# A linear-attention and gated-MLP stack on one core: another opening for the first layer, a later denominator sum, and weight-product rows inside the last q unit

## The chip, the cores and the metric

The kernel runs on one core of one Trainium2 chip. The metric is the device time of one execution in microseconds (us), as a median over runs; the kernel before takes 1659.09 us (three runs, 1657.82 to 1659.62). The profiled execution's span, from its first to its last instruction, is some 2 us shorter than the time of the same run, because the time also covers start and end; spans are compared with spans and times with times. A ratio printed with a result is the mean time of one kernel's runs over the mean of the other's of the same rounds, so it is not quite the ratio of the medians that stand beside it.

Engine names: PE is TensorE (matmuls), PEld its weight load, DVE is VectorE, ACT is ScalarE, POOL is GpSimd, SP issues DMAs. PSUM is the memory that matmuls write to; the kernel cuts it into three "mm" buffers and one "kv" buffer. A "bank" in this text is one of these buffers.

## The reference, cut to what matters

Two kinds of layer alternate, A B A B, on 2048 rows of 1024 bf16 values, with the same weights in both rounds.

```python
x = x + A(layernorm(x), wqkv, wo)      # layer 1, and again layer 3
x = x + B(layernorm(x), w_gate, w_up, w_down)   # layer 2, and again layer 4

# A: linear attention, 32 heads of 32
q, k, v = split(x @ wqkv)
phi = lambda t: where(t > 0, t + 1, exp(t)) + 1e-6
kv = einsum("bhsd,bhse->bhde", phi(k), v);  z = sum_s phi(k)
o  = (phi(q) @ kv) / (phi(q) . z + 1e-6);   return o @ wo

# B:  ((x @ w_gate) * (x @ w_up)) @ w_down        (1024 -> 3584 -> 1024)
```

## The kernel before

The kernel never forms v. It computes G = xᵀ·phi(k) (the "Gram units" g, 32 matmuls each), then kv = wvᵀ·G (the "kv units"), masks kv to the heads' diagonal blocks (KVb), and multiplies it by wo to get one 1024×1024 weight M (eight "rows"). An output unit is then one product of the divided phi(q) with M. The sum z over all rows is gathered by DVE in f32 (`z_unit`), split into two bf16 halves (`z_split`) and summed over the partitions by four matmuls with ones (`z_sum`); ACT copies the result to `zacc`, which every division on DVE reads.

In these traces each engine takes its instructions in program order (the run with the old loads, below, shows DVE idle for 2.48 us in front of a copy that could have run). The order in which these units are called is therefore the schedule:

```python
def phi(ps, dst, scale):                       # after every k and q unit
    nc.scalar.activation(out=e, in_=ps, func=Exp)        # ACT
    nc.scalar.activation(out=dst, in_=ps, func=Relu)     # ACT, then PSUM is free
    nc.vector.tensor_scalar(out=e, in0=e, 1.0, EPS, min, add)   # DVE
    nc.vector.tensor_tensor(out=dst, in0=dst, in1=e, op=add)    # DVE

def m_unit(c):                                  # one row of M
    ps = mm_tile(); both(ps, KVb[:, c, :], wo[c], True, True)   # 2 matmuls
    # copy to M: DVE for odd c, ACT for even c

# opening of layer 1 (turn_pe: transpose by PE, ACT copies one half, turn_rest: DVE the other)
idle(9); ln_stats(0); centre(0); turn_pe(0); idle(2)
ln_stats(1, split=lambda: turn_rest(0)); centre(1)
k_part(0, 0, 4); turn_pe(1); turn_rest(1); k_part(0, 4, 6); k_part(1, 0, 6)
ln_stats(2); centre(2); k_part(0, 6, 8); turn_pe(2); turn_rest(2); k_part(1, 6, 8)
ln_stats(3); centre(3); k_part(2, 0, 4); turn_pe(3); turn_rest(3)
k_part(2, 4, 8); k_part(3, 0, 8)
# ... q and k units with norms between them, z_split last ...

# middle of layers 1 and 3; d(t) is a division, 5 DVE instructions
do([g[0], z_sum, g[1], kv[0]] + d(0) + [g[2], kv[1]] + d(1, 2) + [q[0], g[3], kv[2]] + d(3, 4))
do([q[1], g[4], kv[3]] + d(5, 6) + [q[2], g[5], kv[4]] + d(7))
do(d(8) + [q[3], g[6], kv[5]] + d(9, 10) + [q[4], kv[6], q[5]] + d(11) + [g[7]] + d(12))
do([q[6], kv[7], q[7]])
do([m_unit(c) for c in range(KD)])
do([out_unit(0)] + d(13) + [out_unit(1)] + d(14) + [out_unit(2)] + d(15) + [out_unit(3)])
# ... the other output units, woven with the norms of layer B ...
```

(Arguments shortened; `k_part(t, a, b)` multiplies rows a to b of the key weights into tile t.)

Of the kernel before, what the change touches and what calls it, by code (L numbers as in the profile page):

```python
# [8 lines left out]
ACT = mybir.ActivationFunctionType  # L9
ALU = mybir.AluOpType  # L10
AX = mybir.AxisListType
BF16 = mybir.dt.bfloat16
F32 = mybir.dt.float32
# [13 lines left out]
def kernel(  # L27
# [11 lines left out]
    nc = tc.nc  # L39
# [69 lines left out]
    def load_x(t):  # L109
        load(X[:, t, :], x_view[:, t, :])  # L110

    def load_k(a, b):
        load(wkv[:, a:b, :], wqkv_v[:, a:b, D:2 * D])
# [20 lines left out]
    for c in range(2):  # L134
        load(X[:, 0, c * NB:(c + 1) * NB], x_view[:, 0, c * NB:(c + 1) * NB])
    load_x(1)
    for k in range(4):
        load_k(k, k + 1)
    load_x(2)
    for k in range(4, 8):  # L140
        load_k(k, k + 1)
    load_x(3)
    load_q()
    for t in range(4, NT):
        load_x(t)
# [16 lines left out]
    def mm_tile():  # L162
        return psum.tile([P, 2, NB], F32, tag="mm", bufs=3, name="ps")

    def flat(ps):
        return ps[:].rearrange("p a b -> p (a b)")
# [4 lines left out]
    def idle(n):  # L171
        for _ in range(n):
            nc.tensor.matmul(out=zps[:, 0, :], lhsT=xT[3][:, 0, 0:P], rhs=xT[3][:, 0, :], start=True, stop=True)
# [2 lines left out]

    stat = {}

    def ln_stats(t, split=None):
        st = small.tile([P, 2, 6], F32, tag="st", name="st")  # L180
        for c in range(2):
            nc.vector.bn_stats(out=st[:, c, :], in_=X[:, t, c * NB:(c + 1) * NB])  # L182
            if split and c == 0:
                split()
        mv = small.tile([P, 2], F32, tag="mv", bufs=NT, name="mv")
        nc.vector.bn_aggr(out=mv[:], in_=st[:])  # L186
        ve = small.tile([P, 1], F32, tag="ve", name="ve")
        nc.gpsimd.tensor_scalar(out=ve[:], in0=mv[:, 1:2], scalar1=1e-5, scalar2=None, op0=ALU.add)  # L188
        rstd = small.tile([P, 1], F32, tag="rstd", bufs=NT, name="rstd")
        nc.gpsimd.tensor_tensor(out=rstd[:], in0=ve[:], in1=mhalf[:], op=ALU.pow)  # L190
        stat[t] = (mv, rstd)
# [11 lines left out]
    def both(ps, lhsT, rhs, start, stop):  # L203
        for n in range(2):
            nc.tensor.matmul(out=ps[:, n, :], lhsT=lhsT, rhs=rhs[:, n * NB:(n + 1) * NB], start=start, stop=stop)  # L205

    def phi(ps, dst, scale):
        e = small.tile([P, D], BF16, tag="eb", bufs=3, name="e")
        sc = {} if scale is None else {"scale": scale}
        nc.scalar.activation(out=e[:], in_=flat(ps), func=ACT.Exp, **sc)  # L210
        nc.scalar.activation(out=dst, in_=flat(ps), func=ACT.Relu, **sc)
        nc.vector.tensor_scalar(out=e[:], in0=e[:], scalar1=1.0, scalar2=EPS, op0=ALU.min, op1=ALU.add)  # L212
        nc.vector.tensor_tensor(out=dst, in0=dst, in1=e[:], op=ALU.add)  # L213

    def layer_A(li):
        first = li == 0
# [2 lines left out]
        def scale_of(t):  # L219
            return stat[t][1][:] if first and t < TPG else None  # L220
# [3 lines left out]
        def k_part(t, a, b):  # L224
            if a == 0:
                open_ps[t] = mm_tile()
            ps = open_ps[t]
            tl = t % TPG
            for k in range(a, b):
                both(ps, xT[t // TPG][:, k, tl * P:(tl + 1) * P], wkv[:, k, :], k == 0, k == KD - 1)  # L230
            if b == KD:
                phi(ps, PK[:, t, :], scale_of(t))
# [4 lines left out]
        def q_slot(t):  # L237
            return pq[t if t < 8 else t % 4]

        def q_unit(t):  # L240
            def run():
                ps = mm_tile()
                tl = t % TPG
                for k in range(KD):
                    both(ps, xT[t // TPG][:, k, tl * P:(tl + 1) * P], wq[:, k, :], k == 0, k == KD - 1)
                phi(ps, q_slot(t), scale_of(t))
            return run

        def z_unit(t):
# [51 lines left out]
                                                in1=mask[:].unsqueeze(1).to_broadcast([P, 4, P]), op=ALU.mult)  # L301
            return run

        def m_unit(c):
            def run():
                ps = mm_tile()
                both(ps, KVb[:, c, :], wo[c], True, True)
                if c % 2:
                    nc.vector.tensor_copy(out=M[:, c, :], in_=flat(ps))
                else:  # L310
                    nc.scalar.copy(out=M[:, c, :], in_=flat(ps))
            return run

        def out_unit(t):
            def run():
                ps = mm_tile()
                tl = t % TPG
                for c in range(KD):
                    both(ps, xT[t // TPG][:, c, tl * P:(tl + 1) * P], M[:, c, :], c == 0, c == KD - 1)
                nc.vector.tensor_tensor(out=X[:, t, :], in0=X[:, t, :], in1=flat(ps), op=ALU.add)  # L320
            return run
# [10 lines left out]
            return lambda: [z_unit(t)() for t in ts]  # L332

        if first:
            def centre(t):
                nc.vector.tensor_scalar(out=XN[:, t, :], in0=X[:, t, :], scalar1=stat[t][0][:, 0:1], scalar2=None,
                                        op0=ALU.subtract)

            pts = {}

            def turn_pe(t):
                pt = psum.tile([P, KD, P], BF16, tag="mm", bufs=3, name="pt")
                for k in range(KD):
                    nc.tensor.transpose(out=pt[:, k, :], in_=XN[:, t, k * P:(k + 1) * P], identity=ident[:])
                nc.scalar.copy(out=xT[0][:, 0:4, t * P:(t + 1) * P], in_=pt[:, 0:4, :])  # L345
                pts[t] = pt

            def turn_rest(t):
                nc.vector.tensor_copy(out=xT[0][:, 4:8, t * P:(t + 1) * P], in_=pts[t][:, 4:8, :])

            idle(9)
            ln_stats(0)
            centre(0)
            turn_pe(0)
            idle(2)
            ln_stats(1, split=lambda: turn_rest(0))
            centre(1)
            k_part(0, 0, 4)
            turn_pe(1)
            turn_rest(1)  # L360
            k_part(0, 4, 6)
            k_part(1, 0, 6)
            ln_stats(2)
            centre(2)
            k_part(0, 6, 8)
            turn_pe(2)
            turn_rest(2)
            k_part(1, 6, 8)
            ln_stats(3)
            centre(3)  # L370
            k_part(2, 0, 4)
            turn_pe(3)
            turn_rest(3)
            k_part(2, 4, 8)
            k_part(3, 0, 8)
            for t in range(TPG):
                ln_apply(t, XN[:, t, :])
            main = [q_unit(t) for t in range(4)] + [k_unit(t) for t in range(4, 8)] + [q_unit(t) for t in range(4, 8)]
            main += [k_unit(t) for t in range(8, 16)]
            fill = [norm(t) for t in range(4, 16)]  # L380
            fill += [zs(1, 2), zs(3, 4), zs(5, 6), zs(7), zs(8), zs(9), zs(10, 11), zs(12)]
            do(weave(main, fill))
            do([zs(13, 14, 15), z_split])
        else:
            main = [k_unit(t) for t in range(4)] + [q_unit(t) for t in range(4)]
            main += [k_unit(t) for t in range(4, 8)] + [q_unit(t) for t in range(4, 8)]
            main += [k_unit(t) for t in range(8, 16)]
            fill = [norm(t, False) for t in range(12, 16)]
            fill += [zs(1), zs(2), zs(3)] + [lambda: None] * 2
            fill += [zs(4), zs(5), zs(6), zs(7)] + [lambda: None] * 3 + [zs(8), zs(9), zs(10), zs(11)]  # L390
            do(weave(main, fill))
            do([zs(12, 13, 14, 15), z_split])
        load_v()

        def d(*ts):
            return [div_unit(t) for t in ts]

        g, kv, q = ([f(i) for i in range(KD)] for f in (g_unit, kv_unit, lambda i: q_unit(8 + i)))
        do([g[0], z_sum, g[1], kv[0]] + d(0) + [g[2], kv[1]] + d(1, 2) + [q[0], g[3], kv[2]] + d(3, 4))
        do([q[1], g[4], kv[3]] + d(5, 6) + [q[2], g[5], kv[4]] + d(7))  # L400
        load_o(0)
        load_o(1)
        do(d(8) + [q[3], g[6], kv[5]] + d(9, 10) + [q[4], kv[6], q[5]] + d(11) + [g[7]] + d(12))
        do([q[6], kv[7], q[7]])
        do([m_unit(c) for c in range(KD)])
        load_gu(0)
        load_gu(1)
        load_gu(2)
        for j in DN_ORDER[:2]:
            load_dn(j)  # L410
        do([out_unit(0)] + d(13) + [out_unit(1)] + d(14) + [out_unit(2)] + d(15) + [out_unit(3)])
        for j in DN_ORDER[2:6]:
            load_dn(j)
        fill = [lambda t=t: ln_stats(t) for t in range(4)] + [b_norm(t) for t in range(4)]
        do(weave([out_unit(t) for t in range(4, NT)], fill))
        load_dn(DN_ORDER[6])


# [50 lines left out]
    def do(units):  # L469
        for u in units:  # L470
            u()
# [80 lines left out]
```

## Time and profile before

| | before |
|---|---|
| time, median of 3 | 1659.09 us |
| span of the profiled run | 1657.2 us |
| PE busy | 98% of the span |
| PE waits for the first half of the split of z | 6.7 us, 5.1 of them in layer 1 |
| PE waits for centring, transposed tiles and weight rows in the opening | 5.4 us |
| PE waits in the M product, both layers | 3.5 us |

From the page of the kernel before: the busy time of an engine with its share of the span and its instructions, and the chain of work that ended last.

```profile
PE 1627.2 (98%) x7512; PEld 744.8 (45%) x7663; DVE 607.9 (37%) x889; ACT 286.3 (17%) x384; POOL 54.0 (3%) x141
...
PE 90%; DVE 7%; issue 1%; DMA 1%; POOL 1%; ACT 0%; SPq 0%; DVEq 0%; ACTq 0%
```

PE is the bottleneck and is nearly always busy, so only its holes can be won. The share 98% hides them: the chain of work that ended last is on PE for 90% only, and on DVE for 7%. The holes are in the waits view of the kernel before, PE only; its columns are who waited for whom, us in total, how often, and the longest.

```profile
PE ps L205 <- DVE W L256: 6.7, 2, 5.1
PE pt L344 <- DVE R L336: 3.1, 2, 2.8
PE ps L205 <- ACT PQ L211: 2.3, 2, 1.2
PE ps L205 <- ACT xT L345: 1.7, 2, 1.4
...
PE ps L205 <- DVE W L257: 0.7, 2, 0.6
PE ps L205 <- DVE R L309: 0.6, 2, 0.3
PE ps L205 <- ACT R L311: 0.6, 2, 0.3
```

W L256 and L257 are the two halves of the split of z; R L336 is the centring of a tile in the opening and xT L345 ACT's half of a transposed tile; PQ L211 is the Relu of the last phi(q) before the M rows, R L309 and L311 the copies of M's rows. Where these waits lie is in the timeline of PE in the kernel before (start, duration, line, operands, count, and in brackets the idle time before it and what ended it):

```profile
17.23 1.90 PE L205 MATMUL ps<-W,xT 128*128 128x512 bf16 x8 [1.45 <-ACT xT L345]
21.95 1.03 PE L344 MATMUL pt<-ident,R 128*128 128x128 bf16 x8 [2.81 <-DVE R L336]
...
99.12 7.32 PE L205 MATMUL ps<-R,R 128*128 128x512 bf16 x31
111.58 1.01 PE L205 MATMUL ps<-W,ones 128*128 128x512 bf16 x2 [5.14 <-DVE W L256]
112.74 1.01 PE L205 MATMUL ps<-W,ones 128*128 128x512 bf16 x2 [0.15 <-DVE W L257]
...
122.19 0.61 PE L295 MATMUL kv<-GL,W 128*128 128x128 bf16 x8
...
190.94 0.61 PE L295 MATMUL kv<-GL,W 128*128 128x128 bf16 x8
...
197.02 0.59 PE L205 MATMUL ps<-W,KVb 128*128 128x512 bf16 x2 [1.16 <-ACT PQ L211]
...
257.86 27.79 PE L437 MATMUL ps<-xT,R 128*128 128x512 bf16 x125
```

The first Gram unit starts at 99.12; a kv unit follows at 122.19, 23.1 us later. The first Gram unit's own matmuls take 6.9 us of this. The other 36 matmuls of 512 columns take 0.2157 us each when nothing waits, 7.8 us, but 16.2 us pass. From the last kv unit (190.94) to the first matmul of layer B (257.86) 66.9 us pass for 62.6 us of work.

A hole is followed by a second loss. The windows view of the kernel before, cut where the granted clock changes in the trace: the stretch, its length, busy time of PE and the other engines (instruction counts in brackets), the granted TensorE clock, DMA share and GB/s. The pairs are a stretch of 3.41 us and the one after it.

```profile
18.07:21.48 3.41, 1.06 (x5) 0.29 (x3) 2.60 (x6) 1.13 (x2) 0.03 (x1) 1.00 1.06 387
21.49:24.90 3.41, 2.96 (x13) 1.59 (x14) 0.82 (x2) 0.59 (x1) 1.04 (x2) 0.50 1.03 378
...
110.24:117.06 6.82, 5.33 (x13) 1.85 (x14) 4.57 (x5) 1.01 (x1) 0.00 (x0) 0.50 0.01 4
195.57:198.98 3.41, 1.61 (x7) 0.49 (x6) 2.40 (x4) 3.23 (x4) 0.00 (x0) 1.00 1.07 364
198.99:202.39 3.40, 3.40 (x9) 1.22 (x8) 2.23 (x3) 1.90 (x2) 0.00 (x0) 0.50 1.10 350
```

After a stretch in which PE stood still for half of the time or more, the clock is 0.50 for the next 3.41 us (6.8 us after the long hole at the z sum).

### The profile page before, as it was taken

How to read it: one execution, taken by the hardware profiler on the slowest of the kernel's cores; microseconds unless marked ns; L12 is line 12 of the kernel's file. 1: busy time of each engine (PE TensorE's matmuls, PEld its weight loads, DVE VectorE, ACT ScalarE, POOL GpSimd, SP SyncE). 2: the span in 40 equal slices, each digit the busy share in tenths (PEclk: the TensorE clock that was granted, in tenths of full speed). 3: DMA queues.
4: the chain of work that ended last, by engine and by line, in shares of the span. 5: the costliest groups of instructions: out<-in, count | busy, mean ns of one | idle time of the engine just before them, and what ended most of it. 6: DMA issues, size and time to landing. Idle time of an engine off the chain costs nothing.

```text
span 1657.2 us, 17618 instructions
## 1 busy us (share of the span) xinstructions
PE 1627.2 (98%) x7512; PEld 744.8 (45%) x7663; DVE 607.9 (37%) x889; ACT 286.3 (17%) x384; POOL 54.0 (3%) x141
## 2 busy tenths in 40 slices
PE   8989999999999999999999999999999999999999
PEld 3434444444444444444444444444444444444444
DVE  5797782311321231143345687532113113211111
ACT  4532301100110110011035322011001101100110
POOL 1100000000000000010000000000000000000000
PEclk9999999999999999999999999999999999999999
DMA  6322683630551363043420247555215504521400
GB/s 209 64 64 47 183 247 115 177 115 1 171 159 51 90 175 118 0 153 102 77 76 1 70 96 225 158 156 165 84 64 151 179 26 143 167 84 64 153 0 26
DMA packets 234686, 182.56 MB, mean 110 GB/s; under 512 B 100080, under 2 KB 215408, under 8 KB 234608
## 3 DMA queue, kind: packets, MB, share of 16 engines
q1 hardware_dynamic: 234608, 181.43, 37.5%
q8 instruction: 60, 0.98, 0.2%
q14 instruction: 18, 0.15, 0.0%
HBM read 153.09 MB, written 4.19 MB: 95 GB/s over the span
## 4 chain that ended last, share of the span: by engine, by line
PE 90%; DVE 7%; issue 1%; DMA 1%; POOL 1%; ACT 0%; SPq 0%; DVEq 0%; ACTq 0%
PE ps L437 46%; PE ps L205 42%; DVE GL L252 1%; DVE st L182 1%; PE ps L464 1%; DVE R L213 1%; DVE X L320 0%; DVE den L272 0%; DVE PQ L276 0%; PE kv L295 0%; POOL rstd L190 0%; DVE PQ L213 0%; DVE tmp L270 0%; DVE e L212 0%; DVE R L195 0%
## 5 line engine op out<-in xcount | busy, mean ns | idle before, releaser
L437 PE MATMUL ps<-xT,R 128*128 128x512 bf16 x2380 | 525.8, 379 | 2.8
L437 PEld LDWEIGHTS <-R 128*128 128x128 bf16 x2432 | 238.0, 98 | 287.0
L441 DVE TENSOR_TENSOR R<-gs,ps 128x512 bf16<-128x512 f32 x224 | 153.8, 687 | 533.6 <-ACT gs L440 533.6
L205 PEld LDWEIGHTS <-R 128*128 128x128 bf16 x2248 | 220.4, 98 | 266.6 <-issue 3.1
L440 ACT COPY gs<-ps 128x512 f32<-128x512 f32 x224 | 131.3, 586 | 1044.5 <-PE ps L437 1021.6
L437 PE MATMUL ps<-xT,W 128*128 128x512 bf16 x1133 | 250.6, 379 | 1.0
L205 PEld LDWEIGHTS <-xT 128*128 128x128 bf16 x1536 | 149.8, 98 | 184.2 <-issue 5.3
L205 PE MATMUL ps<-W,xT 128*128 128x512 bf16 x999 | 225.1, 380 | 4.5 <-ACT xT L345 1.7
L437 PEld LDWEIGHTS <-W 128*128 128x128 bf16 x1152 | 112.7, 98 | 135.9
L205 PE MATMUL ps<-W,R 128*128 128x512 bf16 x729 | 169.6, 379 | 0.7
L445 DVE TENSOR_TENSOR X<-X,ps 128x1024 bf16<-128x1024 bf16 (+2 forms) x34 | 39.4, 1158 | 335.9 <-PE ps L205 315.2
L205 PE MATMUL ps<-R,R 128*128 128x512 bf16 x503 | 114.5, 383 | 0.6
L205 PE MATMUL ps<-PQ,R 128*128 128x512 bf16 x484 | 111.5, 379 | 0.6
L205 PE MATMUL ps<-R,xT 128*128 128x512 bf16 x502 | 110.8, 379 | 0.9 <-DVE X L320 0.4
L210 ACT ACTIVATE e<-ps 128x1024 bf16<-128x1024 f32 x56 | 57.4, 1024 | 152.1 <-PE ps L205 150.6
L182 DVE BATCH_NORM_STATS2 st<-X 128x6 f32<-128x512 bf16 x128 | 82.1, 681 | 2.0 <-DMA X<-in_A_x_dram 1.8
L188 POOL TENSOR_SCALAR ve<-mv 128x1 f32<-128x1 f32 x64 | 15.7, 245 | 1362.8 <-DVE mv L186 1362.8
L205 PE MATMUL ps<-xT,R 128*128 128x512 bf16 x243 | 58.2, 379 | 0.3
L205 PE MATMUL ps<-GL,R 128*128 128x512 bf16 x244 | 58.2, 379 | 0.2
L320 DVE TENSOR_TENSOR X<-X,ps 128x1024 bf16<-128x1024 bf16 x32 | 38.5, 1209 | 33.1 <-PE ps L205 30.9
L212 DVE TENSOR_SCALAR e<-e 128x1024 bf16<-128x1024 bf16 x64 | 27.2, 424 | 63.2 <-ACT e L210 63.2
L195 DVE TENSOR_SCALAR R<-X,mv,rstd 128x1024 bf16<-128x1024 bf16 x64 | 33.7, 543 | 36.0 <-POOL rstd L190 36.0
(55 smaller groups left out, 462.9 us busy)
## 6 DMA issues: line engine op xcount, KB each, us to landing
R<-in_B_w_gate_dram SPq DMA_DIRECT2D x38, 1024.0 KB, 5.4
R<-in_B_w_up_dram SPq DMA_DIRECT2D x38, 1024.0 KB, 7.4
W<-in_B_w_gate_dram SPq DMA_DIRECT2D x18, 1024.0 KB, 5.2
W<-in_B_w_up_dram SPq DMA_DIRECT2D x18, 1024.0 KB, 7.2
W<-in_A_wqkv_dram SPq DMA_DIRECT2D x10, 1024.0 KB, 6.8
W<-in_B_w_down_dram SPq DMA_DIRECT2D x6, 1024.0 KB, 11.3
PQ<-in_B_w_down_dram SPq DMA_DIRECT2D x4, 1024.0 KB, 7.9
X<-in_A_x_dram SPq DMA_DIRECT2D x15, 256.0 KB, 5.7
```

The costliest lines, as they stand in the source:

```text
L182: nc.vector.bn_stats(out=st[:, c, :], in_=X[:, t, c * NB:(c + 1) * NB])
L195: nc.vector.tensor_scalar(out=dst, in0=X[:, t, :], scalar1=mv[:, 0:1], scalar2=rstd[:], op0=ALU.subtract, op1=ALU.mult)
L205: nc.tensor.matmul(out=ps[:, n, :], lhsT=lhsT, rhs=rhs[:, n * NB:(n + 1) * NB], start=start, stop=stop)
L210: nc.scalar.activation(out=e[:], in_=flat(ps), func=ACT.Exp, **sc)
L212: nc.vector.tensor_scalar(out=e[:], in0=e[:], scalar1=1.0, scalar2=EPS, op0=ALU.min, op1=ALU.add)
L213: nc.vector.tensor_tensor(out=dst, in0=dst, in1=e[:], op=ALU.add)
L252: nc.vector.tensor_tensor(out=zacc, in0=in0, in1=PK[:, t, :], op=ALU.add)
L320: nc.vector.tensor_tensor(out=X[:, t, :], in0=X[:, t, :], in1=flat(ps), op=ALU.add)
L437: nc.tensor.matmul(out=ps[:, n, :], lhsT=w[:, k, j * P:(j + 1) * P], rhs=xT[g % 2][:, k, :], start=(k == 0), stop=(k == KD - 1))
L440: nc.scalar.copy(out=gs[:], in_=ps[:, 0, :])
L441: nc.vector.tensor_tensor(out=hT[:, f, :], in0=gs[:], in1=ps[:, 1, :], op=ALU.mult)
L445: nc.vector.tensor_tensor(out=X[:, t, a:b], in0=X[:, t, a:b], in1=ps, op=ALU.add)
```

## The change

The intent is to take PE's holes in both attention layers away without adding work.

1. Opening. The third and fourth tiles of x are loaded ahead of some weight rows; the second tile's mean comes from one ACT pass with an accumulator instead of DVE's statistics (which come later); three of the four transposes use the idle kv buffer; and the tiles share each weight row as it lands.
2. `z_sum` is called after the second Gram unit.
3. The rows of M alternate with the rows of the last q unit. This wants the last kv unit one q unit earlier, and the DVE part of the q unit before last put off (`later`).
4. Divisions and q units are spread otherwise.

```diff
+    load_k(0, 1); load_x(2); load_k(1..3); load_x(3); load_k(4..7)      # was: k0..3, x2, k4..7, x3
...
-        do([g[0], z_sum, g[1], kv[0]] + d(0) + [g[2], kv[1]] + d(1, 2) + [q[0], g[3], kv[2]] + d(3, 4))
-        do([q[1], g[4], kv[3]] + d(5, 6) + [q[2], g[5], kv[4]] + d(7))
+        later = []
+        q[6] = q_unit(14, later)
+        do([g[0], g[1], z_sum, kv[0]] + d(0) + [g[2], kv[1]] + d(1, 2) + [g[3], kv[2]] + d(3) + [q[0]] + d(4))
+        do([g[4], kv[3]] + d(5, 6) + [q[1], g[5], kv[4]] + d(7))
...
-        do(d(8) + [q[3], g[6], kv[5]] + d(9, 10) + [q[4], kv[6], q[5]] + d(11) + [g[7]] + d(12))
-        do([q[6], kv[7], q[7]])
-        do([m_unit(c) for c in range(KD)])
+        do(d(8) + [q[2], g[6], kv[5]] + d(9, 10) + [q[3]] + d(11) + [q[4]] + d(12) + [g[7], kv[6], q[5], kv[7], q[6]])
+        q_with_m(15, later)
...
-        do([out_unit(0)] + d(13) + [out_unit(1)] + d(14) + [out_unit(2)] + d(15) + [out_unit(3)])
+        do([out_unit(0)] + d(13) + [out_unit(1), out_unit(2)] + d(14) + [out_unit(3), out_unit(4)] + d(15))
...
+        def q_with_m(t, later):
+            pss = [psum.tile([P, 2, NB], F32, tag="kv", bufs=1, name="pm"), mm_tile()]
+            ps = mm_tile()
+            pss.append(mm_tile())
+            for c in range(KD):
+                pm = pss[(0, 1, 0, 2, 1, 0, 2, 0)[c]]
+                both(pm, KVb[:, c, :], wo[c], True, True)
+                # copy pm to M: ACT for odd c, DVE for even c
+                both(ps, xT[t // TPG][:, c, tl * P:(tl + 1) * P], wq[:, c, :], c == 0, c == KD - 1)
+                if c == 2:
+                    do(later)
+            phi(ps, q_slot(t), scale_of(t))
...
+            idle(9); ln_stats(0); centre(0, stat[0][0][:, 0:1])
+            nc.scalar.activation(out=junk[:], in_=X[:, 1, :], func=ACT.Copy, scale=1.0 / D, accum_out=mean1[:])
+            turn_pe(0); idle(1); centre(1, mean1[:]); turn_pe(1)
+            ln_stats(2); centre(2, ...); turn_rest(0); turn_rest(1)
+            k_part(0, 0, 2); k_part(1, 0, 2); k_part(0, 2, 3); k_part(1, 2, 3)
+            turn_pe(2); k_part(0, 3, 4); k_part(1, 3, 4)
+            ln_stats(3); centre(3, ...); turn_rest(2); ln_stats(1)
+            k_part(2, 0, 4); turn_pe(3); turn_rest(3)
+            k_part(0, 4, 8); k_part(1, 4, 8); k_part(2, 4, 8); k_part(3, 0, 8)
```

(Loads and opening are written several calls to a line here.)

## The prediction

> **What bounds the kernel now.** TensorE: the page has PE busy for 98% of a 1657.2 us span. In the timeline a unit of 16 matmuls of 512 columns takes 3.45 us, 0.2157 us each, which agrees with the Trainium skill, "TensorE: Matmul & The Clock Gate", section "Wait — 56ns, not 53.3ns?" (N/2.4 GHz plus about 2.5 ns). The algorithm's 7464 such matmuls then need 1610 us. The change removes none, so only holes can be won. By the timeline and the waits they are:
>
> 1. Opening: the first four key tiles end at 29.2 us. PE waits for a transposed tile (1.4 us at 17.2) and for the mean-centred fourth tile (2.8 us at 21.95); a clock dip follows (granted 0.83 in 20 to 30).
> 2. Denominator sum, layer 1: PE waits 5.1 us for the split of z, whose DVE chain ends at 112.7. From the end of the first Gram unit (106.1) to that of the first kv unit (122.7) lies 8.2 us of work: 8.3 lost, with a clock dip (0.93 in 100 to 150).
> 3. The same in layer 3: 2.5 us lost.
> 4. Weight product M, both layers: from the last kv unit (190.94; 1006.79) to the first gate matmul (257.86; 1073.71), 66.9 us hold 62.6 of work: 4.35 lost each, behind phi of the last q (waits 1.16, 0.31, 0.33) and in the clock dip after it (0.88, 0.83).
>
> Together 19.5 us besides the opening's 7 to 8.
>
> **What the change does.**
> - Opening: tile 1's mean comes from one ACT pass (about 1.1 us, like an Exp of that size), x2 and x3 load earlier, transposes get the idle kv bank, and the tiles share each weight row as it lands. From the landings (one 256 KB piece per 0.65 to 0.85 us) I get centred tiles at 5.1, 6.1, 8.2 and 11.6 us, the last weight row near 12, and four tiles done at 21.5 to 22.5: 7 us won. The DVE chain of norms (4.1 us per unit against PE's 3.45) shifts with it, so the gain survives.
> - z sum after the second Gram unit: 6.9 us of PE work cover the 5.1 us wait. In layer 1 the z chain and that unit end within 0.3 us of each other, so up to 0.5 may remain. Won: 8 + 2.5.
> - M inside the last q: M copies (ACT 1.02, DVE 1.22 us) alternate with 0.86 us of PE a row; my schedule by hand has no wait over 0.3 us. Won: 4 each, 8.
> - Divisions (4.25 us of DVE each) come later relative to PE. DVE has about 72 us of them and of phi in 76 us of PE before the output units; it just keeps up, some 2 us in hand at the last mask product. Lost: 0 to 2.
>
> **Prediction.** 7 + 8 + 2.5 + 8 - 1 = 24.5 us off: 1634.5 us, range 1631.5 to 1642. Faster by over 2% would need 33 us, more than all holes found: 0.01. Within 2%: 0.98. Slower: 0.01.
>
> **What would show it.** PE's waits for the z split (6.7 us) gone; the clock at 1.00 from 10 us to near the end; four key tiles done before 23 us; the first gate matmul near 239 instead of 257.9; both layers B unchanged; layer 3 some 6 us shorter.
>
> **What would make it wrong.** DVE falling behind in divisions, so that KVb or an output bank is late; the ACT mean later than 6 us; weight rows late because x3 goes ahead of them; a remaining hole long enough for a clock dip.

## The result, and the profile after

The changed kernel takes 1633.56 us (median of 4 runs, 1633.49 to 1633.69) against 1659.10 us; the ratio is 0.9849 (95% interval 0.9834 to 0.9864). Its span is 1631.4 us.

The lines of its page that answer to those of before:

```profile
PE 1617.6 (99%) x7510; PEld 742.8 (46%) x7662; DVE 607.9 (37%) x889; ACT 286.9 (18%) x386; POOL 53.6 (3%) x141
...
PE 98%; DVE 1%; issue 1%; DMA 0%; POOL 0%; ACT 0%; SPq 0%; DVEq 0%
```

The work is as it was, PE is busy 9.6 us less in a span 25.8 us shorter, and the chain of work that ended last is now on PE for 98%. All of PE's waits in the changed kernel, as the waits view has them:

```profile
PE ps L174 <- DVE xT L169: 1.2, 1, 1.2
PE ps L204 <- DMA xT<-R: 0.8, 1, 0.8
PE pt L360 <- DVE R L350: 0.6, 1, 0.6
```

Eight kinds of wait are gone, among them all those for the z split, for phi and for the copies of M. (The view leaves out gaps of 0.15 us or less between the matmuls' modelled ends; such small waits that remain at the first Gram unit and at the start of M are told below.) The first line is the start itself, as before; what is left is 0.6 us in the opening and 0.8 us for one transposed tile among the key units. The timeline of PE in the changed kernel at the same places:

```profile
6.51 0.62 PE L360 MATMUL pt<-ident,R 128*128 128x128 bf16 x8 [0.56 <-DVE R L350]
...
13.04 33.07 PE L204 MATMUL ps<-W,xT 128*128 128x512 bf16 x149
...
91.83 14.15 PE L204 MATMUL ps<-R,R 128*128 128x512 bf16 x63
105.82 1.03 PE L204 MATMUL ps<-W,ones 128*128 128x512 bf16 x4
106.68 0.61 PE L301 MATMUL kv<-GL,W 128*128 128x128 bf16 x8
...
171.97 0.61 PE L301 MATMUL kv<-GL,W 128*128 128x128 bf16 x8
...
176.09 0.60 PE L204 MATMUL pm<-W,KVb 128*128 128x512 bf16 x2
...
178.01 0.59 PE L204 MATMUL pm<-W,KVb 128*128 128x512 bf16 x2
...
238.44 21.75 PE L460 MATMUL ps<-xT,R 128*128 128x512 bf16 x98
```

From 13.04 PE runs without a gap to 46.1, and from 46.92 to the Gram units at 91.83. The z sum comes at 105.82, where the second Gram unit ends, without a wait. M's rows (`pm`, two matmuls) alternate with q rows from 176.09 on. In layer 3 the timeline reads the same.

Cut at these marks (span start, first Gram unit, first kv unit, first matmul of layer B, all read off PE's timeline), the two spans compare stage by stage, in us:

| stage | before | after | won |
|---|---|---|---|
| start to first Gram unit (opening and keys, layer 1) | 99.12 | 91.83 | 7.29 |
| first Gram unit to first kv unit | 23.07 | 14.85 | 8.22 |
| first kv unit to layer B (rest of the middle, M, output) | 135.67 | 131.76 | 3.91 |
| layer 2, and the keys of layer 3 | 663.03 | 663.03 | 0 |
| layer 3: first Gram unit to first kv unit | 17.16 | 14.68 | 2.48 |
| layer 3: first kv unit to layer B | 135.66 | 131.76 | 3.90 |
| layer 4 | 583.5 | 583.5 | 0 |
| span | 1657.2 | 1631.4 | 25.8 |

Stages that the change leaves alone agree to 0.01 us, so this table separates the parts of the change cleanly. It is used for the experiments too.

### The profile page after: what moved, and what is told of

Read it like the earlier page. It is cut to its first block, busy times and chain, and to the rows that moved or that the text cites. A ratio compares the mean times of both kernels' runs of the same rounds, so it can differ in the third digit from the quotient of the medians.

```text
span 1631.4 us, 17617 instructions
## 1 busy us (share of the span) xinstructions
PE 1617.6 (99%) x7510; PEld 742.8 (46%) x7662; DVE 607.9 (37%) x889; ACT 286.9 (18%) x386; POOL 53.6 (3%) x141
## 4 chain that ended last, share of the span: by engine, by line
PE 98%; DVE 1%; issue 1%; DMA 0%; POOL 0%; ACT 0%; SPq 0%; DVEq 0%
PE ps L204 49%; PE ps L460 47%; PE ps L487 1%; PE kv L301 0%; DVE st L183 0%; PE pm L204 0%; DMA xT<-R 0%; DMA X<-in_A_x_dram 0%; DVE PQ L214 0%; POOL rstd L189 0%; DVE R L194 0%; PE pt L360 0%; ACT junk L372 0%; ACT PQ L210 0%; DVE e L213 0%
```

## The experiments

Ten new kernels ran, in three groups on three chips, each group beside runs of the kernel before; all gave correct results. The kernel before took 1657.68 us (median of 7) beside the first group, 1657.19 (7) beside the second, 1658.54 (9) beside the third. The changed kernel itself was run again as the control of the second and third group. Stages as above; L1 and L3 are the layers. Times are medians of 4 or 5 runs, spans are those of the profiled run.

| kernel | time | to Gram L1 | Gram to kv L1 | kv to B L1 | Gram to kv L3 | kv to B L3 |
|---|---|---|---|---|---|---|
| before (first profile) | 1659.09 | 99.12 | 23.07 | 135.67 | 17.16 | 135.66 |
| before + z sum later | 1646.07 | 99.12 | 14.93 | 134.59 | 14.68 | 134.59 |
| before + M inside q | 1651.36 | 99.03 | 22.13 | 132.11 | 17.15 | 132.12 |
| before + opening | 1649.38 | 91.66 | 23.19 | 135.63 | 17.16 | 135.61 |
| before + holes filled | 1653.55 | 98.57 | 21.24 | 134.60 | 17.15 | 134.59 |
| after (control, group 2) | 1633.31 | 91.43 | 15.21 | 131.76 | 14.68 | 131.76 |
| after, old divisions | 1634.38 | 92.06 | 15.12 | 132.10 | 14.68 | 132.11 |
| after, mean by DVE | 1633.77 | 92.23 | 15.21 | 131.76 | 14.68 | 131.76 |
| after, old loads | 1635.90 | 93.25 | 15.25 | 131.76 | 14.68 | 131.76 |
| after (control, group 3) | 1633.50 | 91.58 | 14.98 | 131.76 | 14.67 | 131.76 |
| after, norms ahead | 1632.27 | 90.51 | 14.67 | 131.76 | 14.67 | 131.76 |
| after, M as a block | 1638.22 | 91.35 | 15.21 | 134.06 | 14.67 | 134.06 |
| after, norms ahead and M's start | 1631.29 | 91.02 | 14.67 | 131.35 | 14.67 | 131.35 |

The theory is that the gain is the sum of separate holes in PE's stream, each won by its own part of the change. The main rival is that DVE, which runs at its own pace through norms, z and divisions, gives part of it back.

### One part at a time

**The z sum alone.**

```diff
-        do([g[0], z_sum, g[1], kv[0]] + ...
+        do([g[0], g[1], z_sum, kv[0]] + ...
```

> Kernel before with one edit: the sum of z comes after the second Gram unit, not the first. Theory (holes add up): all of the 8.3 us of layer 1 and the 2.5 us of layer 3 come off, 1648.3 us in all, no wait of PE for the z split, no clock dip near 110. Rival (DVE gives it back): PE runs up against the divisions, which keep their old places, and waits at the mask product or at the output banks; then less than 7 us in all, 1652 or more, with new PE waits for DVE between 170 and 225 us.

1646.07 us (1644.51 to 1646.30), ratio 0.9924. The two stages with the z sum lose 8.14 and 2.48 us, what the whole change won there. The waits view lists no new wait for DVE; the rival falls. But the time is 2.2 us below what was expected: the stages with M, which this kernel does not touch, are 1.08 and 1.07 us shorter as well. The reason is the clock, below.

**M alone.** The diff is that of the change for `phi`, `q_unit` and `q_with_m`, with the old order of divisions but for the end:

```diff
-        ... + d(9, 10) + [q[4], kv[6], q[5]] + d(11) + [g[7]] + d(12))
-        do([q[6], kv[7], q[7]])
-        do([m_unit(c) for c in range(KD)])
+        ... + d(9, 10) + [q[4]] + d(11) + [g[7]] + d(12) + [kv[6], q[5], kv[7], q[6]])
+        q_with_m(15, later)
```

> Kernel before with M's rows inside the last q unit (and the order of the last q and kv units that this needs); opening, z sum and the divisions' order stay. Theory: 4 to 4.35 us off in each of the layers 1 and 3, 1650.5 us in all, clock dips near 199 and 1015 gone. Rival: the copies of M collide with the phi of the q before and half of it comes back as PE waits on banks, 1655.

1651.36 us (1650.31 to 1651.84), ratio 0.9957. The stage from kv to B is 3.56 us shorter in layer 1 and 3.54 in layer 3, a little under the 4 expected; about 1.07 us of it is the clock dip that no longer comes (below). No wait on a bank for phi is left in it, so the rival falls too; the missing third of a microsecond per layer belongs to the divisions, below.

**The opening alone.** The diff is that of the change for loads, `ln_stats` and the opening.

> Kernel before with the new opening alone. Theory: the DVE chain to the z split shifts with PE, so the whole 7.4 us by which the fourth key tile ends earlier in the changed kernel's trace reach the end: 1651.7 us. Rival: the z chain, which follows DVE's own pace, does not move, and the wait for it grows by what the opening won: 1657 or more, and a PE wait for the z split of 10 us or more in layer 1.

1649.38 us (1648.99 to 1651.66), ratio 0.9949. The first stage is 7.46 us shorter. The wait for the z split is 5.1 us, as in the kernel before, not 10: DVE's chain to z moves with PE, so the opening's gain is kept. The median lies 2.3 us under the expected 1651.7, which was counted from 1659.1; the kernel before took 1657.68 on this chip, and the mean clock of 0.996 to 0.998 in these four runs tells of fewer dips in most.

**The divisions.** The changed kernel with the order of divisions and q units of the kernel before:

```diff
-        do([g[0], g[1], z_sum, kv[0]] + ... + [g[3], kv[2]] + d(3) + [q[0]] + d(4))
+        do([g[0], g[1], z_sum, kv[0]] + ... + [q[0], g[3], kv[2]] + d(3, 4))
...
-        do([out_unit(0)] + d(13) + [out_unit(1), out_unit(2)] + d(14) + [out_unit(3), out_unit(4)] + d(15))
+        do([out_unit(0)] + d(13) + [out_unit(1)] + d(14) + [out_unit(2)] + d(15) + [out_unit(3)])
```

> The changed kernel with the divisions and q units in the order of the kernel before (new opening, z sum and M stay). Theory: with PE further ahead, the old order makes an output bank wait for a division, 0.4 to 1 us in each of the two layers: 1634.4 to 1635.6 us, PE waits for DVE in the line of the output add. Rival: the new spread does nothing, 1633.6.

1634.38 us (1633.95 to 1634.94) against the control's 1633.31 (1633.02 to 1633.48). The stage from kv to B costs 0.34 us more in layer 1 and 0.35 in layer 3. The waits view of this kernel names about 0.2 us of it in each, for the output add on DVE that frees a bank:

```profile
PE ps L204 <- DVE X L334: 0.4, 2, 0.2
```

So part 4 of the change is worth 0.7 us; the rest of the 1.07 us between the medians lies in the opening, which is the same code in both and varies by some tenths from run to run (91.43 to 91.83 in three profiles of the changed kernel, 92.06 in this one).

### How much of it was the clock

The holes of the kernel before, filled with matmuls whose result nobody reads. They leave the holes as long as they are, but keep PE busy:

```diff
+    def busy(n, tag):            # n idle matmuls into the free kv buffer
+        t = psum.tile([P, 2, NB], F32, tag="kv", bufs=1, name="fz")
+        for _ in range(n):
+            nc.tensor.matmul(out=t[:, 0, :], lhsT=ones[:], rhs=X[:, 0, 0:NB], start=True, stop=True)
...  z_sum:    +  busy(25 if first else 7, 'kv')
...  m_unit:   +  busy((0, 0, 6, 2, 2)[c], 'kv')       # for c in 2, 3, 4
...  opening:  +  busy(13, 'kv')                        # before turn_pe(3)
```

> Kernel before, with idle matmuls on operands that are there put into its holes: 13 before the fourth transpose of the opening, 25 (layer 1) and 7 (layer 3) before the z sum, 6, 2 and 2 before the third to fifth row of M. The holes stay as long as they are, only the clock stays up. It measures what part of the gain was the clock. Theory: a dip costs half of the time that PE worked in it, 1.5 in the opening, 2.6 at the z sum, 1.6 at each M, 7.3 us together: 1651.8 us, and the clock at 1.00 throughout. Rival 1: the dips lie inside the waits and cost nothing, 1659. Rival 2: the idle matmuls outlast the holes and cost what they save.

1653.55 us (1653.29 to 1654.56) against 1657.68, ratio 0.9971, and the granted clock is 1.00 throughout. Both rivals fall, but the theory had the size wrong: by the stages, the dips cost 0.55 us before the first Gram unit, 1.83 at the z sum of layer 1 and 1.07 at each M, 4.5 us together where 7.3 was expected. In the M stage, for one, eight matmuls take 3.47 us at half clock and 2.28 at full clock (below), not half of 3.47: at full clock PE waits for the copies instead.

The dips also explain why the kernel before scatters and the changed one does not. Over the 23 runs of the kernel before beside the three groups, the time follows the mean granted clock of the run: 1653.91 us at 0.999, 1655.28 at 0.998, 1656.57 to 1657.74 at 0.996 and 0.997, 1658.46 to 1659.97 at 0.995. The one run almost without dips took 1653.91 us, just what the kernel with the filled holes takes. The changed kernel was at 1.00 in all its runs, and these spread over 0.6 us or less on a chip.

Why did the later z sum also take the dips at M away? In that kernel the waits at M are as long as before. Its PE timeline, first row after the Relu of phi(q):

```profile
188.88 0.59 PE L205 MATMUL ps<-W,KVb 128*128 128x512 bf16 x2 [1.16 <-ACT PQ L211]
189.78 0.59 PE L205 MATMUL ps<-W,KVb 128*128 128x512 bf16 x2 [0.31 <-ACT R L311]
190.70 2.28 PE L205 MATMUL ps<-PQ,KVb 128*128 128x512 bf16 x8 [0.33 <-DVE R L309]
```

The waits are 1.16, 0.31 and 0.33 us as before, but the eight matmuls of the later rows take 2.28 us here and took 3.47 in the kernel before at half clock. Its windows view, cut on a grid of 3.413 us (the shortest dip's length) that starts where the clock last changed:

```profile
185.36:188.77 3.41, 2.35 (x11) 0.98 (x10) 1.92 (x4) 1.88 (x3) 0.00 (x0) 1.00 0.94 235
188.78:192.18 3.40, 2.52 (x10) 0.96 (x10) 3.32 (x4) 2.72 (x4) 0.00 (x0) 1.00 1.08 365
192.19:195.60 3.41, 3.35 (x16) 1.36 (x14) 2.02 (x2) 1.16 (x2) 0.00 (x0) 1.00 1.10 348
```

In the kernel before all three waits fell into one such stretch (PE busy 1.61 of 3.41 us, shown above), and the clock was halved in the next. Here the grid's edge falls between the first wait and the others, PE is busy 2.35 and 2.52 us of two stretches, and nothing happens. The kernel before has the same contrast within one execution, in layer 3. The two waits at its z sum, 1.58 and 0.57 us, are longer together than the three at M (1.16, 0.31, 0.32), but an edge of the grid falls between them (the first two rows); the waits at M lie in one stretch (the third row), and only there does the clock fall:

```profile
926.02:929.43 3.41, 1.94 (x10) 0.69 (x7) 3.28 (x4) 1.01 (x1) 0.00 (x0) 1.00 0.21 80
929.44:932.84 3.40, 2.72 (x12) 1.20 (x13) 1.67 (x2) 1.01 (x1) 0.00 (x0) 1.00 0.00 0
1011.36:1014.76 3.40, 1.60 (x7) 0.52 (x6) 2.33 (x4) 3.29 (x4) 0.00 (x0) 1.00 1.05 359
1014.77:1018.17 3.40, 3.40 (x9) 1.23 (x9) 2.27 (x2) 1.76 (x2) 0.00 (x0) 0.50 1.12 356
```

The Trainium skill, "TensorE: Matmul & The Clock Gate", section "What's actually happening", has it that the activity window is 3413 ns long and free-running. These traces agree in length: in each of the fourteen kept ones all changes of the clock lie whole multiples of 3.4133 us apart. Cut on these grids, they hold some 6650 stretches at full clock. The ten with PE busy for 1.69 us or less were each followed by 0.50, and none of the others, from 1.79 us up, was. So in these traces the limit lies between 1.69 and 1.79 us of busy time, about half of a stretch.

No run set the grid on purpose, so the part that the place on the grid plays is read off these traces. It fits that the dips of one and the same kernel change from run to run: the four runs of the opening-only kernel have mean clocks from 0.996 to 0.998. By the mean clock (0.999 or more) each run of the kernel with the later z sum had at most one dip of 3.41 us, and in the profiled one it lies in the opening. An estimate from this trace makes M without a dip the likelier case: of all places that the grid could take, only about 18% put under 1.7 us of PE's work into one stretch there. So these 1.07 us per layer are not a sure gain of that edit. Why M dipped more often in the kernel before stays open. In the changed kernel's trace no stretch of that length that starts between 5 and 1620 us has PE busy for less than 2.6 us, so by this limit no place of the grid would give a dip.

### The opening's parts

**The mean by DVE.**

```diff
-            nc.scalar.activation(out=junk[:], in_=X[:, 1, :], func=ACT.Copy, scale=1.0 / D, accum_out=mean1[:])
-            centre(1, mean1[:])
+            ln_stats(1)
+            centre(1, stat[1][0][:, 0:1])
```

> The changed kernel, but the second tile's mean comes from DVE's statistics as before, not from ACT. Theory: the second centred tile comes 0.65 us later (1.3 + 0.2 us of statistics after the first tile's centring instead of a wait for ACT) and the whole kernel ends 0.65 us later, 1634.2. Rival: the rows of the weights bound the opening, and it makes no difference, 1633.6.

1633.77 us (1633.73 to 1633.97) against 1633.31 (1633.02 to 1633.48): 0.46 us, where 0.65 was expected. The ranges are apart, so the ACT pass is worth about half a microsecond.

**The old order of loads.**

```diff
-    x1, k0, x2, k1, k2, k3, x3, k4..k7
+    x1, k0, k1, k2, k3, x2, k4..k7, x3
```

> The changed kernel with the loads of the opening in the old order (the third tile after four weight rows, the fourth after eight). Theory: the fourth tile lands about 2.6 us later, its centring ends near 13.7 instead of 11.6 us and PE waits 1 to 1.5 us for it: 1634.6 to 1635.1. Rival: weight rows that land earlier make up for it, 1633.6 or less.

1635.90 us (1635.33 to 1636.97): 2.6 us worse by the medians, 1.9 in the profiled run's span, so more than the 1.0 to 1.5 expected. The theory was right that the loads matter, but not about which tile. PE's timeline in this kernel:

```profile
10.92 0.61 PE L359 MATMUL pt<-ident,R 128*128 128x128 bf16 x8 [1.43 <-DVE xT L363]
...
14.38 0.61 PE L359 MATMUL pt<-ident,R 128*128 128x128 bf16 x8 [0.26 <-DVE xT L363]
```

PE loses 1.43 us at the transposes of the third tile, and only 0.26 at the fourth. It waits there for DVE's copy of the first tile out of the kv buffer (`turn_rest`), and this copy stands in DVE's program behind the statistics of the third tile, which wait for its landing: DVE is idle for 2.48 us before them in this trace. A late load thus stopped PE through a copy that had nothing to do with it, because DVE works in order.

### Order or alternation

The rows of M as a block between the last two q units, all else as in the changed kernel:

```diff
             for c in range(KD):
                 both(pm, KVb[:, c, :], wo[c], True, True)
                 # copy
-                both(ps, xT..., wq[:, c, :], c == 0, c == KD - 1)
+            for c in range(KD):
+                both(ps, xT..., wq[:, c, :], c == 0, c == KD - 1)
```

> The changed kernel with the rows of M as one block between the last two q units instead of alternating with the last q's rows; the order of units, banks and copies stays. It parts the two halves of the M change: order of units, and alternation. Theory: the copies (ACT 1.02 us, after 2.05 us of phi; DVE 1.23 us) take 5 to 6 us for a block that PE does in 3.45, so PE waits 1.5 to 2 us for banks in each layer: 1636.5 to 1637.5 us, and a clock dip may follow. Rival: only the order of the units counted, 1633.6.

1638.22 us (1637.72 to 1639.30) against 1633.50: 4.7 us worse, 2.30 in each layer, a little above the expected 1.5 to 2. The waits view of this kernel shows PE before the copies of M's rows:

```profile
PE pm L204 <- DVE R L322: 2.5, 4, 0.9
PE pm L204 <- ACT R L320: 1.3, 2, 0.7
```

So with the new order of units alone 1.6 of the 3.9 us per layer are won (135.67 against 134.06), and the alternation earns the other 2.3. But 1.07 of the 1.6 is the clock dip, which this kernel does not have: against 134.60 with the filled holes the order itself is worth 0.5. As for the alternation, a row of M needs 0.43 us of PE but 1.02 (ACT) or 1.23 us (DVE) to be copied, and a q row between two M rows gives the copies the time. The clock stayed at 1.00; no dip followed.

### What was left

In layer 1, DVE still holds PE up a little. In the first Gram unit PE waits for DVE's sum of the last phi(k), 0.18 us in the changed kernel's first profile and more in the control of the second group, whose timeline has it as

```profile
98.44 7.50 PE L204 MATMUL ps<-R,R 128*128 128x512 bf16 x34 [0.37 <-DVE R L214]
```

There PE reached the Gram units 0.4 us earlier (91.43 against 91.83), yet the first kv unit starts at 106.64 against 106.68: DVE gave that much of the opening back. So layer 1's stage took 14.85 to 15.21 us in three profiles of the changed kernel, and layer 3's 14.68 or 14.67.

The changed kernel's trace also leaves PE 0.81 us of waiting for a transposed tile, and twice 0.4 us at the start of M: its first row starts at 176.09, 0.23 us after the q unit before it ends (172.41 and 3.45), because the mask product on DVE ended only at 176.03, behind the sum of phi; and its third row starts at 178.01 instead of 177.82, because it waits for the buffer of the first. Two kernels go after these.

```diff
 # norms one tile ahead (both kernels)
+            ln_stats(4)                       # in place of the scaling of tiles 0 to 3
+            def ahead(t):   # in place of norm(t)
+                    if t + 1 < NT: ln_stats(t + 1)
+                    ln_apply(t, XN[:, t, :]); turn(XN[:, t, :], t // TPG, t % TPG)
+                    if 8 <= t < 12: ln_apply(t - 8, XN[:, t - 8, :])
 # M's start (second kernel only)
+        sum5 = []; q[5] = q_unit(13, sum5)
-        ... [g[7], kv[6], q[5], kv[7], q[6]])
+        ... [g[7], kv[6], q[5], kv[7], lambda: do(sum5), q[6]])
+        # q rows after M's row c: 0 | 1, 2 | 3 | 4 | 5 | 6 | 7 | none
```

> The changed kernel with the norms of layer 1 one tile ahead (the statistics of a tile are taken before the tile in front of it is scaled, so DVE no longer waits 1.0 us for GpSimd at each tile), and the scaling of the first four tiles moved behind. Theory: the last PE wait of the key stage that the changed kernel's trace shows (0.81 us, for a transposed tile) goes, and the z chain ends early enough not to take its place: 0.8 us off, 1632.6. Rival: the wait turns up again at the z split, no gain.

> The norms one tile ahead as above, and M's start mended: the sum of phi of the q unit before moves behind the mask product (the mask product held up M's first row by 0.23 us), and two q rows stand between M's second and third row (its third row waited 0.19 us for the bank of the first). Theory: 0.8 us and twice 0.4 us off, 1631.8 us, faster than both kernels. Rival: the waits only move on, 1632.6.

Norms ahead: 1632.27 us (1631.93 to 1632.77), 1.2 us less than the control where 0.8 was expected. Besides the wait for the transposed tile, the one for the last phi(k) is gone: layer 1's stage at the z sum takes 14.67 us as layer 3's does, not 14.98. Both together: 1631.29 us (1631.08 to 1631.48) against the control's 1633.50 (1633.28 to 1633.82) on the same chip, 2.2 us less, and a ratio of 0.9841 to the kernel before. It beats both kernels; its ranges do not touch the control's. Each M stage is 0.41 us shorter. The waits view of the second kernel shows all that PE still waits for:

```profile
PE ps L174 <- DVE xT L169: 1.2, 1, 1.2
PE pt L361 <- DVE R L351: 0.3, 1, 0.3
```

The first is the start; the second is the second tile's centring in the opening.

The control, as expected before its two runs:

> The changed kernel as it is, as the control for the runs beside it on this chip: 1633.6 us, within 0.3.

> The changed kernel once more, as the control on this chip: 1633.3 to 1633.6 us.

## Why the prediction was right

- **Size.** 1634.5 us was predicted, 1633.56 measured, inside the range of 1631.5 to 1642. The forecast was a sum of holes that the timeline of the kernel before shows, with a deduction of 1 us for what DVE might give back. Without the deduction it would have been off by less than 0.1 us, but such closeness is luck: the gain was 25.5 us by the medians on this chip, 23.9 and 25.0 beside the second and third group, because the kernel before moves with its dips.
- **Opening, 7 us.** Measured 7.29 (7.46 alone). The centred tiles were forecast at 5.1, 6.1, 8.2 and 11.6 us and ended at 5.0, 6.5, 8.5 and 11.6; the four key tiles were forecast at 21.5 to 22.5 and end just before 21.87, where the last one's Exp starts. That DVE's chain of norms moves along was right, by the opening-only run, up to some tenths of a us (the wait for the last phi(k)). Not foreseen as a cost, though its forerunner was in the trace of before: PE's 0.8 us wait for a transposed tile stays.
- **z sum, 8 and 2.5 us.** Measured 8.22 and 2.48. The margin in layer 1 was as narrow as said: the z split ends at 105.33 and the second Gram unit at 105.82. The up to 0.5 us that might remain turned up in another place, the last phi(k) in the first Gram unit: 0.18 us here, 0.3 and 0.5 more than layer 3's stage in the two controls.
- **M, 4 us each.** Measured 3.91 and 3.90. "my schedule by hand has no wait over 0.3 us" held: its two waits were 0.23 and 0.19 us.
- **Divisions, 0 to 2 us lost.** Nothing was lost. The about 2 us in hand at the last mask product are there (DVE idles 2.04 us before the sum of phi that stands ahead of it). The new spread of the last divisions is what keeps it so: with the old one 0.35 us per layer are lost. The deduction of 1 us was thus too much.
- **Clock.** It is 1.00 from 10 us to the end, as forecast. Each dip's cost was counted inside its hole, which made the sum right; when it was estimated by itself, for the filled holes, it came out at 7.3 us where the run showed 4.5.
- **The marks.** Waits for the z split gone; the first gate matmul at 238.44 (forecast 239); both layers B unchanged to 0.01 us; layer 3's attention 6.38 us shorter (forecast about 6).

## What to carry to other kernels

When one engine is busy for 98%, list its idle gaps by place and by what ended them, and price a stage as the time between two marks minus the work in it: that includes the clock dip which a wait alone does not show, and the sum of such prices was right here to 1 us in 26. Put a short product that waits for another engine behind the next long independent one, and let products that PE makes faster than they can be copied out alternate with rows of a long accumulation. Engines that work in order pass delays on: a late load held PE through an unrelated copy that stood behind it.

## What the Trainium skill lacked or had wrong

- "TensorE: Matmul & The Clock Gate", section "HAM oscillation — how this bites in real kernels", gives the rule of no PE-idle gaps over about 3.4 us. It is too weak: here the clock fell to 0.50 for 3.41 us after a stretch of 3.41 us in which PE was busy for 1.61 us and its longest single wait was 1.16 us. With 2.35 and 2.52 us busy in two neighbouring stretches it did not fall. Over all kept traces, 1.69 us busy was the most before a fall and 1.79 the least without one. The section "A second HAM failure mode: psum-queue depth-cycling" of that page does say that frequent short idles trip the clock too, but gives no size for them.
- The same page has the window's phase vary from run to run, at a kernel's start. No page says that this scatters the time of a kernel with mid-sized holes: 1653.9 to 1660.0 us for the kernel before, along with its mean clock, against 0.6 us or less on a chip for the one without holes.
- "ScalarE: Activation LUTs" names the accumulator output but not that it costs a second instruction: after the pass over 128x1024 bf16, 1.06 us, the reading of the accumulator took 0.18 us.
